# Softmax sums in an attention and two-layer MLP kernel: transposed before VectorE inverts them, with a new table of planned times

## The chip, the cores and the metric

The kernel runs on one core of a Trainium2 chip. The metric is the device time of one execution in microseconds (us). TensorE (PE in the profile) multiplies matrices, VectorE (DVE), ScalarE (ACT) and GpSimd (POOL) work on elements, SyncE (SP) issues the DMAs.

## What is computed

Attention over 4 batches x 8 heads, 576 positions, head size 64, with a rotary embedding on q and k; then two dense layers with their own activations, 2304 tokens, model width 512, inner width 2048.

```python
scores = scale * q_rot @ k_rot.T
scores = scores - max(scores, axis=-1)
attn = exp(scores)
attn = attn / (sum(attn, axis=-1) + 1e-09)
x = (attn @ v) reshaped to [2304, 512]
h = x @ w_in;   x = (h - tanh(h)) @ w_out
h = x @ w2_in;  out = (h * sigmoid(1.702 * h)) @ w2_out
```

All is float32; each product is made of products of rounded high and low parts, so most operands are split into two tiles.

## The kernel before

**Attention.** Heads are worked on in 16 pairs. For each pair, GpSimd makes the rotary embedding of q and k in four passes over a 128x1152 tile (`rope`, L484 and L486, and `qk_lo`, L527), and SP copies the halves to where TensorE wants them. Scores come in 9 units (`scores`, L561) into two PSUM tiles `sp`. VectorE takes the row maximum of each (`rowmax`, L567), ScalarE the exponential and, in the same instruction, the row sum (`expo`, L573), which goes to one column of the tile `sum`, 128 rows by 9 columns for a pair. TensorE transposes the exponentials (`etrans`, L591 to L604); ScalarE casts each transposed block to its high part (`evac`, L626, tile `eh`), VectorE subtracts that from the block and gets the low part (L624, tile `el` or a part of `eh`). TensorE multiplies both with v (`pv`, L640), ScalarE or VectorE copies the result out of PSUM (`pv_out`, L649 and L651, tile `xt`), and SP stores it.

**The sums.** The output is not divided at once. Five steps make the factor 1 / (sum + 1e-9) of every row and store it in DRAM: `r_add` (L664, ScalarE, adds 1e-9 to the 128x9 tile), `r_inv` (L667, VectorE, inverts it), `r_trans` (L671, TensorE, transposes it to 9x128 in the PSUM tile `ps_r`), `r_copy` (L677 on VectorE or L679 on ScalarE, copies it to the tile `rw`), `r_save` (L685 and L686, three DMAs to `rs`). Much later `x_fetch` (L862) reads the factors back, spread over partitions, and GpSimd multiplies the attention's output with them (L874) while it makes the first layer's input.

**The dense layers.** From about 282 us on, TensorE works through the two layers: `up` (L836), `down` (L941), and the second layer's products (L1138, L1179, L1265, L1322), with the activations on ScalarE and VectorE and the splits of their results on GpSimd. The weights of the first layer are converted from 64-bit words on the way (L325, L334, L336, L341, L345), partly during attention.

**What sets the order.** Every step is an `op` with a priority, the engines that may run it with a modelled duration, what it reads and writes, and the buffers it holds. The planner (`Plan.order`) runs them through a model of the engines before the program is traced, and the order that comes out is fixed: each instruction is held behind the one before it on its engine. The priorities of the steps of pair n are `PER * n + OFF[step]`; those of the first eight weight conversions are in `CT`. An op with `port=True` on VectorE is kept from overlapping GpSimd's in the model; others are not.

Of the kernel before, what the change touches and what calls it, by code (L numbers as in the profile page):

```python
# [34 lines left out]
}  # L35
PER = 14.87
# [11 lines left out]
CT = (41.4, 75, 90, 105, 120, 135, 150, 159.7)  # L48
# [149 lines left out]
def _cost(eng, dur):  # L198
    return eng, dur - LAP[eng], dur
# [3 lines left out]
def attention_moe_kernel(ctx: ExitStack, tc, qk, v, w1_in, w1_out, w2_in, w2_out, rope_tab, eye, out):  # L203
# [273 lines left out]
    def engine():  # L477
        return nc.vector if cur[0].eng == "DVE" else nc.gpsimd
# [184 lines left out]
    def r_add(n):  # L663
        nc.scalar.activation(st["sum", n], st["sum", n], AF.Identity, bias=1e-9)  # L664

    def r_inv(n):
        nc.vector.reciprocal(st["sum", n], st["sum", n])  # L667
# [5 lines left out]
    def r_copy(n):  # L673
        rw = st["rw", n] = ap.tile([9, 128], F32, tag="rw", name="rw", bufs=1)
        p = st.pop(("rt", n))[0:9, 0:128]
        if cur[0].eng == "DVE":
            nc.vector.tensor_copy(rw, p)  # L677
        else:
            nc.scalar.copy(rw, p)  # L679
# [43 lines left out]
    for n in range(NP):  # L723
        t0 = PER * n

        def at(k):
            return t0 + OFF[k]

        def bind(fn, *a, n=n):
            return lambda: fn(n, *a)  # L730
# [64 lines left out]
        for h in range(2):  # L795
            for part in range(2):
# [6 lines left out]
                for stage in range(3):  # L803
# [3 lines left out]
                    if stage == 0:  # L807
# [10 lines left out]
        op(at("rt"), bind(r_add), [_cost("ACT", 0.23)], [("e", n, i) for i in range(9)], [("ra", n)], [("sum", n)])  # L818
        op(at("rt"), bind(r_inv), [_cost("DVE", 0.215)], [("ra", n)], [("ri", n)], [("sum", n)])
        op(at("rt"), bind(r_trans), [("PE", 0.11, 0.27)], [("ri", n), "ident"], [("rt", n)], [("bank", "r", n), ("sum", n)])  # L820
        late_ops.append(op(at("rt"), bind(r_copy), [_cost("ACT", 0.25), _cost("DVE", 0.25)], [("rt", n)], [("rw", n)],
                           [("bank", "r", n), ("rw", n)]))
# [764 lines left out]
```

## Time and profile before

| | |
|---|---|
| median of 3 runs | 1064.37 us (1063.09 to 1064.77) |
| the profiled execution's own time | 1063.46 us |
| its span, first to last instruction | 1061.7 us |
| busy: PE, DVE, ACT, POOL | 98%, 65%, 68%, 73% of the span |
| granted TensorE clock | 0.999 |

Busy time is the union of an engine's instructions. A matmul's end is modelled and overlaps the next one, so a busy PE is not PE at its peak. A share over the whole span mixes attention, where all engines work, with the dense layers, where PE alone is full: read the stages apart.

### The profile page before, as it was taken

To read this page: it belongs to the slowest core of one execution; us is meant where nothing else is said; L and a number is where in the kernel's file an instruction comes from. 1 tells how busy PE (TensorE), PEld (TensorE's weight loads), DVE (VectorE), ACT (ScalarE), POOL (GpSimd) and SP (SyncE) were. 2 spreads that over 40 slices of the span, in tenths; PEclk is the share of its full clock that TensorE was granted. 3 is DMA by queue.
4 is the path that set the end of the run, shared out by engine and by line. 5 is a ranking of instruction groups with operands and counts; after the bars stand their busy time and mean duration, and the time that the engine had idled before them with its cause. 6 is when DMAs were issued, how large, how long until landed. Compare 5 with 4: busy or idle time off the path is not lost.

```text
span 1061.7 us, 19352 instructions
## 1 busy us (share of the span) xinstructions
PE 1038.3 (98%) x6578; PEld 998.7 (94%) x6578; DVE 693.8 (65%) x1243; ACT 719.7 (68%) x1623; POOL 780.1 (73%) x667
## 2 busy tenths in 40 slices
PE   5999999999999999999999999999999999999998
PEld 3898899998999999999999999998888999999998
DVE  7899898899787887777677776654121333562335
ACT  5999999989887776667767776743545444544442
POOL 2888899989356669869978868933933779977763
PEclk9999999999999999999999999999999999999999
DMA  8868778768433326655756578487468676777621
GB/s 280 281 237 308 260 277 281 259 224 294 152 99 120 105 96 214 209 193 191 243 189 227 189 259 308 156 308 280 157 221 340 233 291 224 263 283 266 232 99 60
DMA packets 107188, 236.36 MB, mean 223 GB/s; under 512 B 11729, under 2 KB 61137, under 8 KB 100049
## 3 DMA queue, kind: packets, MB, share of 16 engines
q1 hardware_dynamic: 107088, 235.12, 63.8%
q8 instruction: 52, 0.85, 0.3%
q14 instruction: 48, 0.39, 0.1%
HBM read 157.42 MB, written 49.36 MB: 195 GB/s over the span
## 4 chain that ended last, share of the span: by engine, by line
PE 77%; DVE 7%; ACT 5%; POOL 4%; DMA 3%; issue 3%; SPq 1%; DVEq 0%; ACTq 0%; POOLq 0%
PE ps_h L836 18%; PE y L941 18%; PE ps_h L1138 17%; PE y L1265 10%; PE y L1179 6%; DVE mx L567 2%; PE sp L561 2%; DVE el L624 2%; ACT e L573 2%; PE ps_o L640 2%; PE y L1322 2%; POOL qk L484 1%; PE ps_e L598 1%; ACT eh L626 1%; DMA st<-in_moe_w_out_dram 1%
## 5 line engine op out<-in xcount | busy, mean ns | idle before, releaser
L836 PE MATMUL ps_h<-xh,w 128*128 128x384 f32 x768 | 210.8, 336 | 0.2 <-ACT u L906 0.2
L1138 PE MATMUL ps_h<-xo,ws 128*128 128x384 f32 x1008 | 201.3, 341 | 0.0
L941 PE MATMUL y<-gh,w 128*128 128x384 f32 x768 | 195.6, 336 | 0.0
L1138 PEld LDWEIGHTS ps_h<-xo,ws 128*128 128x128 f32 x1008 | 173.5, 188 | 8.1 <-ACT su L1148 2.1
L836 PEld LDWEIGHTS ps_h<-xh,w 128*128 128x128 f32 x768 | 140.1, 188 | 0.7 <-ACT u L906 0.5
L941 PEld LDWEIGHTS y<-gh,w 128*128 128x128 f32 x768 | 139.0, 188 | 0.0
L928 POOL TENSOR_TENSOR gl<-t,gh 128x384 fp32r<-128x384 f32 x96 | 97.8, 1019 | 42.7 <-ACT gh L926 33.9
L941 PE MATMUL y<-gl,w 128*128 128x384 f32 x384 | 129.0, 336 | 0.0
L836 PE MATMUL ps_h<-xl,w 128*128 128x384 f32 x384 | 128.8, 335 | 0.0
L1296 DVE TENSOR_TENSOR sum<-y,sum 128x256 f32<-128x256 f32 (+1 forms) x108 | 54.0, 537 | 112.8 <-PE y L1265 112.8
L561 PE MATMUL sp<-kt,qt 128*128 128x288 f32 x624 | 115.8, 313 | 1.5 <-ACT e L573 0.9
L573 ACT ACTIVATE e<-sp,mx 128x576 f32<-128x576 f32 x144 | 107.5, 747 | 12.8 <-DVE mx L567 11.6
L567 DVE TENSOR_REDUCE mx<-sp 128x1 f32<-128x576 f32 x144 | 107.2, 748 | 4.8 <-PE sp L561 3.2
L624 DVE TENSOR_TENSOR el<-ps_e,eh 128x512 fp32r<-128x512 f32 x144 | 96.5, 684 | 14.3 <-ACT eh L626 13.4
L626 ACT CAST eh<-ps_e 128x512 fp32r<-128x512 f32 (+2 forms) x208 | 101.7, 532 | 4.6 <-PE ps_e L602 2.0
L910 DVE SCALAR_TENSOR_TENSOR w<-z,ps_h 128x384 f32<-128x384 f32 x96 | 52.8, 550 | 78.5 <-ACT t L903 78.2
L926 ACT CAST gh<-t 128x384 fp32r<-128x384 f32 x96 | 49.3, 513 | 70.9 <-DVE t L918 60.7
L561 PEld LDWEIGHTS sp<-kt,qt 128*128 128x128 f32 x624 | 87.9, 189 | 9.1 <-ACT e L573 7.7
L640 PE MATMUL ps_o<-eh,vw 128*128 128x256 f32 (+1 forms) x320 | 91.1, 307 | 3.5 <-DVE el L624 2.6
L1400 POOL TENSOR_TENSOR ex<-t,g2h 128x384 fp32r<-128x384 f32 x72 | 72.2, 1019 | 25.3 <-ACT g2h L1397 25.3
L1265 PE MATMUL y<-ws,g2h 128*128 128x256 f32 x486 | 90.1, 283 | 0.0
L1265 PE MATMUL y<-ws,ex 128*128 128x256 f32 x345 | 80.7, 282 | 0.0
(143 smaller groups left out, 2525.0 us busy)
## 6 DMA issues: line engine op xcount, KB each, us to landing
ws<-w SPq DMA_DIRECT2D x48, 1024.0 KB
w<-part SPq DMA_DIRECT2D x40, 512.0 KB
kt<-qk SPq DMA_DIRECT2D x64, 288.0 KB
ws<-w SPq DMA_DIRECT2D x24, 768.0 KB
qk<-in_qk_dram SPq DMA_DIRECT2D x30, 576.0 KB
st<-in_moe_w_in_dram SPq DMA_DIRECT2D x32, 512.0 KB
st<-in_moe_w_out_dram SPq DMA_DIRECT2D x32, 512.0 KB
qt<-qk SPq DMA_DIRECT2D x64, 144.0 KB
```

The source lines that it names most:

```text
L561: nc.tensor.matmul(sp[:, half, 0:HS], lhsT=w, rhs=m[:, half * HS:(half + 1) * HS], start=(o == 0), stop=(o == len(ops) - 1))
L567: nc.vector.tensor_reduce(mx, st["sp", n, i], axis=AX.XY, op=ALU.max, negate=True)
L573: nc.scalar.activation(e.rearrange("p (a b) -> p a b", a=2), st.pop(("sp", n, i)), AF.Exp, bias=st.pop(("mx", n, i)), accum_out=st["sum", ...
L624: nc.vector.tensor_sub(lo, src, hi.bitcast(F32))
L626: nc.scalar.copy(hi, src)
L640: nc.tensor.matmul(p[:, 0:wd], lhsT=w[:, h, kc].rearrange("p d a -> p (d a)"), rhs=m, start=(o == 0), stop=(o == 8))
L836: nc.tensor.matmul(p, lhsT=wi[:, a, kk, :], rhs=xx[:, kk, :], start=(o == 0), stop=(o == 11))
L928: nc.gpsimd.tensor_sub(gs[i][1], g, gs[i][0].bitcast(F32))
L941: nc.tensor.matmul(y, lhsT=w[:, a, cols], rhs=g, start=first and o == 0, stop=last and o == 2)
L1138: nc.tensor.matmul(hq[q, b], lhsT=wt(lw, k), rhs=x[:, 2 * lx + k], start=n in (1, 7) and c == 0, stop=n in (2, 3, 4) and c == 5, skip_grou ...
L1265: nc.tensor.matmul(y[:, x:x + 256], lhsT=g[:, cols], rhs=ws[q, s][:, a + l, o:o + 256], start=not own and m == 0, stop=m == 2 and (not own ...
L1400: engine().tensor_sub(l, g, h.bitcast(F32))
```

## The change

The sums are transposed first, and VectorE inverts the 9x128 tile from PSUM straight into `rw`. The copy is gone. The addition of 1e-9 may now run on VectorE too. The tables `OFF`, `PER` and `CT` have other numbers; two lines of them are shown.

```diff
-    "pv01": 23.03, "pv11": 27.36, "pv10": 29.03, "rt": 26.05, "dx": 25.11,
+    "pv00": 18.99, "pv01": 22.94, "pv11": 27.46, "pv10": 31.19, "rt": 18.15, "dx": 22.0,
...
-PER = 14.87
+PER = 14.83
...
-CT = (41.4, 75, 90, 105, 120, 135, 150, 159.7)
+CT = (52.6, 76.2, 89.5, 91.8, 122.9, 134.7, 153.2, 166.8)
...
     def r_add(n):
-        nc.scalar.activation(st["sum", n], st["sum", n], AF.Identity, bias=1e-9)
-
-    def r_inv(n):
-        nc.vector.reciprocal(st["sum", n], st["sum", n])
+        if cur[0].eng == "ACT":
+            nc.scalar.activation(st["sum", n], st["sum", n], AF.Identity, bias=1e-9)
+        else:
+            engine().tensor_scalar(st["sum", n], st["sum", n], 1.0, 1e-9, op0=ALU.mult, op1=ALU.add)
 
     def r_trans(n):
         p = st["rt", n] = bank(("bank", "r", n), "ps_r")
         nc.tensor.transpose(p[0:9, 0:128], st["sum", n], ident)
 
-    def r_copy(n):
+    def r_inv(n):
         rw = st["rw", n] = ap.tile([9, 128], F32, tag="rw", name="rw", bufs=1)
-        p = st.pop(("rt", n))[0:9, 0:128]
-        if cur[0].eng == "DVE":
-            nc.vector.tensor_copy(rw, p)
-        else:
-            nc.scalar.copy(rw, p)
+        nc.vector.reciprocal(rw, st.pop(("rt", n))[0:9, 0:128])
...
-        op(at("rt"), bind(r_add), [_cost("ACT", 0.23)], [("e", n, i) for i in range(9)], [("ra", n)], [("sum", n)])
-        op(at("rt"), bind(r_inv), [_cost("DVE", 0.215)], [("ra", n)], [("ri", n)], [("sum", n)])
-        op(at("rt"), bind(r_trans), [("PE", 0.11, 0.27)], [("ri", n), "ident"], [("rt", n)], [("bank", "r", n), ("sum", n)])
-        late_ops.append(op(at("rt"), bind(r_copy), [_cost("ACT", 0.25), _cost("DVE", 0.25)], [("rt", n)], [("rw", n)],
-                           [("bank", "r", n), ("rw", n)]))
+        op(at("rt"), bind(r_add), [_cost("DVE", 0.15), _cost("ACT", 0.22)], [("e", n, i) for i in range(9)], [("ra", n)], [("sum", n)])
+        op(at("rt"), bind(r_trans), [("PE", 0.11, 0.27)], [("ra", n), "ident"], [("rt", n)], [("bank", "r", n), ("sum", n)])
+        late_ops.append(op(at("rt"), bind(r_inv), [_cost("DVE", 0.28)], [("rt", n)], [("rw", n)], [("bank", "r", n), ("rw", n)]))
```

Because the planner runs anew, all engines have another order; the first 30 rows of VectorE's and of ScalarE's are the same as before. Over the whole program the instructions of the engines are the same but for these: on VectorE, 16 inversions of 128x9 become 16 of 9x128, 2 copies of `rw` go, 15 additions come, and 24 copies of `xt` become 30 (14 to 16 of 128x256, 10 to 14 of 128x320); on ScalarE, 16 additions become 1, 14 copies of `rw` go, 40 copies of `xt` become 34 (18 to 16 and 22 to 18), and 6 casts of `vw` 128x640 become 8; on GpSimd 10 roundings of `vw` become 8.

On VectorE in the eighth pair, before: the tile `sum_1981` holds the pair's sums, `mx` is a row maximum over a score tile `sp`, `el` and `eh` are the low parts of transposed blocks.

```order
L624 TENSOR_TENSOR el_2127<-ps_e_2221,eh_2126 128x2x256
L567 TENSOR_REDUCE mx_2255<-sp_2238 128x1
L624 TENSOR_TENSOR eh_2243<-ps_e_2234,eh_2243 64x256
L667 RECIPROCAL sum_1981<-sum_1981 128x9
L567 TENSOR_REDUCE mx_2281<-sp_2263 128x1
L624 TENSOR_TENSOR el_2244<-ps_e_2275,eh_2243 128x512
```

VectorE touches the sums once. The same place after the change, where `sum_1979` are the sums and `rw_2227` the factors:

```order
L624 TENSOR_TENSOR el_2120<-ps_e_2176,eh_2119 128x4x128
L667 TENSOR_SCALAR sum_1979<-sum_1979 128x9
L649 COPY xt_2214<-ps_o_2186 128x256
L624 TENSOR_TENSOR eh_2119<-ps_e_2193,eh_2119 64x256
L675 RECIPROCAL rw_2227<-ps_r_2217 9x128
L567 TENSOR_REDUCE mx_2229<-sp_2207 128x1
L567 TENSOR_REDUCE mx_2245<-sp_2220 128x1
L624 TENSOR_TENSOR el_2120<-ps_e_2231,eh_2119 128x2x256
```

VectorE now touches them twice, two instructions apart, and both row maxima of the score tiles in flight stand behind the inversion. TensorE in the same pair, before:

```order
L598 MATMUL ps_e_2315<-ident_84,e_2218 128x128
L671 MATMUL ps_r_2323<-ident_84,sum_1981 9x128
L561 MATMUL sp_2326<-kt_1999,qt0_135 128x288 x8
L561 MATMUL sp_2342<-kt_1999,qt0_135 128x288 x4
L640 MATMUL ps_o_2354<-eh_2126,vw_1923 128x320
```

The transposition of the sums came after the blocks `ps_e` of the next units. TensorE after the change:

```order
L640 MATMUL ps_o_2186<-eh_2019,vw_1921 128x256
L561 MATMUL sp_2207<-kt_2009,qt0_135 128x288 x4
L671 MATMUL ps_r_2217<-ident_84,sum_1979 9x128
L561 MATMUL sp_2220<-kt_2009,qt0_135 128x288 x4
L598 MATMUL ps_e_2231<-ident_84,e_2108 128x128
```

It stands now between the two score units whose row maxima stand behind the inversion on VectorE.

## Rows read from the trace of the kernel before

**Rows 1.** The page, section 1: busy us of each engine over the span.

```profile
PE 1038.3 (98%) x6578; PEld 998.7 (94%) x6578; DVE 693.8 (65%) x1243; ACT 719.7 (68%) x1623; POOL 780.1 (73%) x667
```

**Rows 2.** Windows: stretch, length, busy us of PE, PEld, DVE, ACT, POOL; clock, DMA.

```profile
20.00:282.00 262.00, 254.33 (x1908) 235.73 (x1908) 234.97 (x398) 245.36 (x602) 222.86 (x126) 1.00 0.77 263
282.00:1040.00 758.00, 757.76 (x4514) 740.57 (x4513) 430.64 (x790) 461.76 (x997) 549.54 (x533) 1.00 0.61 212
```

**Rows 3.** Windows again, the densest 40 us of VectorE's share in attention.

```profile
40.00:80.00 40.00, 38.64 (x300) 36.54 (x300) 36.42 (x62) 38.22 (x93) 33.60 (x16) 1.00 0.73 253
```

**Rows 4.** Waits of VectorE, 20 to 282 us: total, times, longest (us).

```profile
DVE el L624 <- ACT eh L626: 12.6, 29, 0.9
DVE eh L624 <- ACT eh L626: 5.3, 7, 1.4
```

**Rows 5.** Waits of ScalarE, 20 to 282 us.

```profile
ACT e L573 <- DVE mx L567: 10.7, 28, 0.8
```

**Rows 6.** Groups of VectorE by form: count | busy us, mean ns | idle before.

```profile
L567 DVE TENSOR_REDUCE mx<-sp 128x1 f32<-128x576 f32 x144 | 107.2, 748 | 4.8 <-PE sp L561 3.2
...
L649 DVE COPY xt<-ps_o 128x256 f32<-128x256 f32 x14 | 5.8, 416 | 0.1
...
L649 DVE COPY xt<-ps_o 128x320 f32<-128x320 f32 x10 | 4.8, 476 | 0.0
...
L667 DVE RECIPROCAL sum<-sum 128x9 f32<-128x9 f32 x16 | 3.4, 212 | 0.3
...
L677 DVE COPY rw<-ps_r 9x128 f32<-9x128 f32 x2 | 0.5, 274 | 0.0
...
L449 DVE CAST qt<-zero 128x128 fp32r<-128x128 f32 x2 | 0.4, 223 | 0.0
L519 DVE TENSOR_REDUCE even<-ident 128x1 f32<-128x64 f32 x1 | 0.2, 210 | 0.0
```

**Rows 7.** Groups of ScalarE by form, 20 to 290 us.

```profile
L651 ACT COPY xt<-ps_o 128x320 f32<-128x320 f32 x22 | 9.3, 421 | 0.6 <-PE ps_o L640 0.2
...
L651 ACT COPY xt<-ps_o 128x256 f32<-128x256 f32 x18 | 6.7, 374 | 0.3 <-PE ps_o L640 0.3
...
L490 ACT CAST vw<-v 128x640 fp32r<-128x640 f32 x5 | 4.0, 795 | 0.0
L679 ACT COPY rw<-ps_r 9x128 f32<-9x128 f32 x14 | 3.5, 253 | 1.5 <-PE ps_r L671 1.4
L664 ACT ACTIVATE sum<-sum 128x9 f32<-128x9 f32 x16 | 3.4, 215 | 0.0
```

**Rows 8.** Timeline of VectorE around one inversion: start, length.

```profile
166.03 0.22 DVE L667 RECIPROCAL sum<-sum 128x9 f32<-128x9 f32 x1
166.16 0.70 DVE L567 TENSOR_REDUCE mx<-sp 128x1 f32<-128x576 f32 x1
```

**Rows 9.** Groups of GpSimd by form, 20 to 282 us.

```profile
L484 POOL TENSOR_TENSOR qk<-qk,tab 128x1152 f32<-128x1152 f32 x28 | 74.2, 2667 | 3.8 <-PE ps_e L598 2.0 <-DMA v<-in_v_dram 1.4
L486 POOL TENSOR_TENSOR qk<-qk 128x1152 f32<-128x1152 f32 x15 | 39.9, 2663 | 18.2 <-DVE qk L484 17.2
L527 POOL TENSOR_TENSOR qk<-qk 128x1152 fp32r<-128x1152 f32 x14 | 37.4, 2670 | 4.1 <-ACT qk L490 4.1
L546 POOL TENSOR_TENSOR vw<-v,vw 128x640 fp32r<-128x640 f32 x16 | 25.4, 1589 | 4.6 <-ACT vw L490 4.0
```

**Rows 10.** Timeline at 724 us: VectorE's instructions with two SBUF inputs beside GpSimd's.

```profile
723.84 0.41 DVE L1200 TENSOR_TENSOR tt<-tt 128x256 f32<-128x256 f32 x1
724.12 1.01 POOL L1167 TENSOR_TENSOR g2l<-t,g2h 128x384 fp32r<-128x384 f32 x1 [0.74 <-ACT g2h L1165]
724.18 1.23 DVE L1202 TENSOR_TENSOR tt<-tt 128x256 f32<-128x256 f32 x1
```

**Rows 11.** One line's instructions: ns min/median/max, first and last start.

```profile
L667 DVE RECIPROCAL sum<-sum x16: 202/215/217, 33.5 to 281.2; 128x9 f32<-128x9 f32 x16
```

**Rows 12.** The first layer's up products: ns min/median/max, first and last start.

```profile
L836 PE MATMUL ps_h<-xh,w x768: 334/336/440, 281.9 to 679.0; 128*128 128x384 f32 x192
```

8 rows, old and new, of the table OFF are left out of this document.

## The prediction

> **What bounds the kernel now.** The page first: over the whole span TensorE is 98% busy and no other engine above 73% [rows 1], which suggests that nothing on VectorE matters. The windows say otherwise [rows 2]. From 282 to 1040 us TensorE is busy 757.76 of 758 us: a wall, whose length this change does not touch, so whatever moves its start moves the end by as much. From 20 to 282 us, the attention, three engines are almost full together: ScalarE 245.36 of 262 us (93.6%), VectorE 234.97 (89.7%), GpSimd 222.86 (85%), and TensorE's 254.33 has the ends of matmuls modelled into it. The question is how long these 262 us become.
>
> The waits say how the engines hold each other. VectorE's idle time is 262 - 234.97 = 27 us, and 12.6 + 5.3 = 17.9 us of it is waiting for ScalarE's casts [rows 4]. ScalarE waits 10.7 us for row maxima of VectorE [rows 5]. So the two feed each other in a loop, and each is the late one at times. The first 20 us are the same in both orders but for a swap or two, and I leave them out.
>
> **The change part by part.** All durations are from the profiled execution; sums are made against its 1063.46 us, 0.91 us under the median of the three runs, 1064.37 us.
>
> *ScalarE loses work.* 15 additions go at 0.215 us, 14 copies of the factors at 0.253, 2 copies of xt at 0.374 and 4 at 0.421, and 2 casts of 128x640 come at 0.795 [rows 7]: -3.23 - 3.54 - 0.75 - 1.68 + 1.59 = **-7.6 us**, so 237.8 us remain. GpSimd loses two short roundings; I count nothing for it.
>
> *VectorE: what has a price in the rows.* 16 inversions of 128x9 go at 0.212 us, 2 copies at 0.274, and 2 + 4 copies of xt come at 0.416 and 0.476 [rows 6]: -3.39 - 0.55 + 2.74 = -1.2 us.
>
> *VectorE: the inversion of 9x128.* No row has it. The lower bound is the copy of the same shape from PSUM, 0.274 us. The upper one is the old inversion scaled by columns, 0.212 x 128 / 9 = 3.0 us. To choose I take the old one apart. The two reductions give VectorE's price per column: (748 - 210) / (576 - 64) = 1.05 ns, and 210 - 64 x 1.05 = 143 ns on top [rows 6]. The copy of 9x128 fits that (143 + 134 = 277 against 274), and so do the copies of 256 columns (143 + 269 = 412 against 416). The inversion does not: by that rate its 9 columns are worth 152 ns and it took 212. The 69 ns above the 143 are 7.7 ns a column. So 128 columns are an estimated 143 + 128 x 7.7 = **1.13 us**, four times the copy, and 16 of them 18.1 us. The reading against it is that a very short instruction has a floor near 0.21 us whatever it does; no row of VectorE has fewer than 64 columns beside this one, so that stays open and is a rival.
>
> [...]
>
> *VectorE: the addition.* One input and the output in SBUF, 9 columns: 143 + 9 x 1.05 = 0.152 us, 15 of them 2.3 us, if nothing holds it. The bound on the other side is a wait for GpSimd, which is a rival below.
>
> *Sum on VectorE.* -1.2 + 18.1 + 2.3 = +19.2 us of durations. An instruction's last part lies under the next one's first: the inversion is 0.22 us long, and its successor starts 0.13 us after it [rows 8], 0.08 to 0.09 us of overlap. There are 21 more instructions, so the busy time grows by 19.2 - 21 x 0.085 = **+17.4 us, to 252.4 us of 262**.
>
> *The wait that is added.* The inversion now waits for TensorE's transposition, and that for VectorE's addition, with one or two of VectorE's instructions between (in the eighth pair a copy of 0.416 us [rows 6] and one low part). Queued behind the inversion are the maxima of both score tiles in flight; ScalarE's exponentials wait for these, and the tiles are free for TensorE only then. So the extra microsecond falls where it stops three engines, not in a corner. The lower bound of its own price is nothing, where the transposition is in time; I put nothing in the sum for it, since VectorE's fullness below has room for such gaps. On SP the three DMAs per pair that store the factors stay, in other places; what reads them is GpSimd's multiplication, pairs later, so I cost that at nothing. If it were late, GpSimd, with 39 us idle in the stretch, would take it.
>
> *From load to time.* VectorE becomes the fullest engine. The fullest one of before, ScalarE, came to 93.6% of the stretch, the rest being waits that the loop needs. If VectorE packs as well, the stretch is 252.4 / 0.936 = 269.7 us, 7.7 more. Bounds: if it only packs as in its own densest 40 us, 36.42 of 40 [rows 3], it is 252.4 / 0.91 = 277, 15 more; if the new work falls wholly into its waits, 0. I take 7.7, since ScalarE's share is the one that a limiting engine has reached over the whole stretch. For the new order itself I put nothing: it was made with 0.28 us for the inversion. **Forecast: 1063.46 + 7.7 = 1071.0 us, rounded, with 1066 to 1078 as its own range.**
>
> **The rivals.**
>
> *The addition waits for GpSimd: 1082 us.* What the trace shows: at 724.18 us an instruction of VectorE with two SBUF inputs began 0.06 us after one of GpSimd's and took 1.23 us, where its like took 0.41 alone [rows 10]. The old inversion, with one SBUF input, was never held: 202 to 217 ns in 16 instances beside a busy GpSimd [rows 11]. The addition has one input as well, which speaks against. [...] GpSimd's 57 instructions of 2.67 us and 16 of 1.59 [rows 9] hold 58% and 10% of the 262 us; who comes at a random moment waits half their length, 0.58 x 1.33 + 0.10 x 0.79 = 0.85 us on average, and about 0.1 more for the shorter kinds. 15 x 0.94 = 14 us on VectorE. With half of it in idle time that is 1078, in full 1086.
>
> [...]
>
> *The inversion costs what the copy does: 1060 us, faster.* With the floor reading it is 0.274 us and VectorE grows by 17.4 - 16 x 0.86 = 3.7 us only, to 238.7, beside ScalarE's 237.8. The fullest engine then has 6.7 us less than before; by the same 93.6% the stretch is 255 us, 7 us shorter, and half of that, 1060, if waits rather than load decide. The point where it turns is a VectorE as full as ScalarE was, 245.4 us: 7 us less than I have, so an inversion of 0.69 us.
>
> *VectorE's waits swallow it: 1064 us, no change.* The 17.9 us that VectorE waits for casts shrink as ScalarE gets lighter, and 17.4 us of work fit in their place. Against it: the inversion sits in front of the maxima, not where the waits were.
>
> **How the numbers follow.** Forecast 0.45, wait for GpSimd 0.25, cheap inversion 0.17, swallowed 0.13. Slower by over 0.2% (2.1 us, about what a measurement of this kernel tells from no change): the first two, 0.70; same 0.13; faster 0.17. The range, 1060 to 1083 us, holds the forecast, the swallowed case and about half of each of the other two.
>
> **What would show it.** The inversion's group on VectorE: 1.1 us right, 0.3 wrong. Its busy time in attention: about 252 us, ScalarE's about 238, with ScalarE waiting longer for maxima than the 10.7 us of before. The addition's group: 0.15 us, or a median near 1 us with a maximum above 2 for the rival. The first up product, at 281.9 us now [rows 12], at about 289. The forecast is wrong if the inversion is long and that product starts no later.

## The result

The changed kernel takes 1079.45 us (median of 4 runs, 1078.69 to 1080.1), the kernel before beside it 1064.51 (1063.09 to 1064.77). The ratio is 1.0147, with a 95% interval of 1.0134 to 1.016: 15 us slower. The forecast was 7.5 us slower. The rival with the wait for GpSimd stood at 1082, which is the forecast's long inversion with the wait on top. Both happened.

The page of the changed kernel, span and section 1 (busy us of each engine over the span), answers to [rows 1]:

```profile
span 1077.9 us, 19392 instructions
...
PE 1042.9 (97%) x6578; PEld 1000.9 (93%) x6578; DVE 718.5 (67%) x1264; ACT 716.6 (66%) x1592; POOL 774.7 (72%) x661
```

VectorE has 718.5 - 693.8 = 24.7 us more work than before, ScalarE 3.1 less, and the span is 16.2 us longer. Where it grew is told by one line's first start, as in [rows 12], here of the changed kernel (ns min/median/max, first and last start):

```profile
L830 PE MATMUL ps_h<-xh,w x768: 334/336/445, 297.3 to 694.4; 128*128 128x384 f32 x192
```

The first up product begins at 297.3 us in place of 281.9, so 15.4 of the 16.2 us are lost in the attention. The windows agree with [rows 2] on the rest: TensorE is as full after 282 us as it was.

```profile
20.00:282.00 262.00, 243.39 (x1794) 224.22 (x1794) 242.45 (x392) 225.52 (x533) 215.49 (x118) 0.99 0.74 254
282.00:1040.00 758.00, 757.21 (x4515) 738.08 (x4514) 442.32 (x808) 471.32 (x1021) 540.54 (x523) 1.00 0.62 215
```

In the first window ScalarE, which was at 245.36 us, does only 225.52, and VectorE is now the fullest of the three that work on elements. The two new instructions of VectorE, each as one line's instructions. The addition is shown with those who waited for it (us, times):

```profile
L667 DVE TENSOR_SCALAR sum<-sum x15: 173/668/2082, 30.8 to 276.8; 128x9 f32<-128x9 f32 x15
...
  PE ps_r L671: 7.6, 11
  PEld ps_r L671: 5.0, 4
```

The inversion is shown with what VectorE waited for before it:

```profile
L675 DVE RECIPROCAL rw<-ps_r x16: 935/946/947, 32.4 to 295.3; 9x128 f32<-9x128 f32 x16
...
  PE ps_r L671: 0.2, 1
```

The inversion takes 935 to 947 ns in its 16 instances. The addition takes 173 at best and 2082 at worst, with the same tile of 128x9 each time. The group by form gives the sum of both over 20 to 282 us (busy us, mean ns):

```profile
L675 DVE RECIPROCAL rw<-ps_r 9x128 f32<-9x128 f32 x15 | 14.1, 941 | 0.5
L667 DVE TENSOR_SCALAR sum<-sum 128x9 f32<-128x9 f32 x15 | 11.7, 779 | 0.3
```

Unhindered, the 15 additions would be 15 x 0.174 = 2.6 us, so 11.7 - 2.6 = 9.1 us of them are waiting. For whom, the timeline shows at the longest one, VectorE first, then GpSimd (start, length):

```profile
224.35 0.41 DVE L649 COPY xt<-ps_o 128x256 f32<-128x256 f32 x1
224.85 2.08 DVE L667 TENSOR_SCALAR sum<-sum 128x9 f32<-128x9 f32 x1
226.97 0.42 DVE L624 TENSOR_TENSOR eh<-ps_e,eh 64x256 fp32r<-64x256 f32 x1
227.41 0.95 DVE L675 RECIPROCAL rw<-ps_r 9x128 f32<-9x128 f32 x1
```

```profile
224.29 2.62 POOL L527 TENSOR_TENSOR qk<-qk 128x1152 fp32r<-128x1152 f32 x1
226.87 0.99 POOL L872 TENSOR_TENSOR xl<-x,xh 128x384 fp32r<-128x384 f32 x1
```

GpSimd's rounding began 0.56 us before the addition and ended at 224.29 + 2.62 = 226.91; the addition ended at 224.85 + 2.08 = 226.93. It waited out the rest of GpSimd's instruction, though it has only one input. The timelines show the same for all 15: 11 additions began while a GpSimd instruction ran and ended 28 to 34 ns after that instruction did. Three met none, and one met the last 19 ns of one; these four took 173 to 175 ns.

The transposition of the sums on TensorE stood behind the addition. From the longest one, two stretches of the windows, in the order of [rows 2]:

```profile
225.10:226.99 1.89, 0.00 (x2) 0.00 (x1) 1.86 (x2) 0.87 (x2) 1.89 (x2) 1.00 0.12 25
227.16:230.57 3.41, 3.41 (x16) 3.30 (x16) 3.35 (x6) 1.83 (x5) 3.41 (x3) 0.50 0.67 254
```

TensorE did nothing for 1.89 us, and then its granted clock was 0.50 for 3.41 us. From 104.28 us on it was 0.50 for 3.41 us again, after 1.61 us in which TensorE did nothing (101.53 to 103.14) and the second longest addition (1966 ns) ended. In the kernel before the clock is 1.00 up to 1059.3 us, 2.4 us before its end. What these two falls cost was not measured by themselves; half of 2 x 3.41 us, 3.4 us of TensorE's time, is an estimate of the most.

The waits of ScalarE, 20 to 282 us, before and after, answer to [rows 5]:

```profile
ACT e L573 <- DVE mx L567: 10.7, 28, 0.8
ACT eh L626 <- PE ps_e L598: 1.6, 3, 1.1
ACT eh L626 <- PE ps_e L602: 1.6, 3, 0.7
```

```profile
ACT e L573 <- DVE mx L567: 20.5, 24, 3.0
ACT eh L626 <- PE ps_e L598: 7.0, 10, 1.3
ACT eh L626 <- PE ps_e L602: 6.0, 5, 2.8
```

Those of VectorE after the change answer to [rows 4]:

```profile
DVE el L624 <- ACT eh L626: 8.4, 15, 0.9
...
DVE eh L624 <- ACT eh L626: 1.3, 2, 1.0
```

ScalarE waits 20.5 us for row maxima in place of 10.7, and 13.0 us for TensorE's transposed blocks in place of 3.2. VectorE waits 9.7 us for casts in place of 17.9. The account of VectorE goes by the stretch from 20 us to the first up product. Before:

```profile
20.00:281.90 261.90, 254.23 (x1908) 235.63 (x1907) 234.97 (x398) 245.26 (x601) 222.76 (x126) 1.00 0.77 263
```

After:

```profile
20.00:297.30 277.30, 258.35 (x1908) 238.08 (x1908) 256.76 (x415) 239.16 (x568) 221.24 (x124) 0.99 0.72 246
```

VectorE has 21.8 us more work in it and is idle for 20.5 us in place of 26.9. So 21.8 - 6.4 = 15.4 us remain, the delay of the first up product. The other 2.9 of its 24.7 us lie behind it, where TensorE is full.

### The profile page after: what moved, and what is told of

The parts are those of the page before. It is cut to its first block, busy times and chain, and to the rows that moved or that the text cites. A ratio compares the mean times of both kernels' runs of the same rounds, so it can differ in the third digit from the quotient of the medians.

```text
span 1077.9 us, 19392 instructions
## 1 busy us (share of the span) xinstructions
PE 1042.9 (97%) x6578; PEld 1000.9 (93%) x6578; DVE 718.5 (67%) x1264; ACT 716.6 (66%) x1592; POOL 774.7 (72%) x661
## 5 line engine op out<-in xcount | busy, mean ns | idle before, releaser
L573 ACT ACTIVATE e<-sp,mx 128x576 f32<-128x576 f32 x144 | 107.5, 748 | 23.8 <-DVE mx L567 22.4
L626 ACT CAST eh<-ps_e 128x512 fp32r<-128x512 f32 (+2 forms) x208 | 103.7, 528 | 14.3 <-PE ps_e L598 7.3
L640 PE MATMUL ps_o<-eh,vw 128*128 128x256 f32 (+1 forms) x320 | 94.9, 315 | 1.9 <-DVE rw L675 1.7
L1394 POOL TENSOR_TENSOR ex<-t,g2h 128x384 fp32r<-128x384 f32 x71 | 71.6, 1021 | 23.8 <-ACT g2h L1391 23.8
```

What stands on the lines that cost most here:

```text
L573: nc.scalar.activation(e.rearrange("p (a b) -> p a b", a=2), st.pop(("sp", n, i)), AF.Exp, bias=st.pop(("mx", n, i)), accum_out=st["sum", ...
L626: nc.scalar.copy(hi, src)
L640: nc.tensor.matmul(p[:, 0:wd], lhsT=w[:, h, kc].rearrange("p d a -> p (d a)"), rhs=m, start=(o == 0), stop=(o == 8))
L1394: engine().tensor_sub(l, g, h.bitcast(F32))
```

## The experiments

Theory A: the addition's wait for GpSimd makes the loss. Theory B: the longer inversion makes it. Theory C: the new order, with the added hop from VectorE to TensorE and back, makes it. The first four runs keep the order of the change, instruction by instruction, on every engine, and change only what the addition or the inversion is (the last leaves the addition out). The kernel before took 1064.04 us in them.

**An addition that does not wait** (`e1_add_one_port`).

```diff
-            engine().tensor_scalar(st["sum", n], st["sum", n], 1.0, 1e-9, op0=ALU.mult, op1=ALU.add)
+            nc.vector.tensor_reduce(st["sum", n], st["sum", n].rearrange("p (a one) -> p a one", one=1), axis=AX.X, op=ALU.add)
```

> The addition on VectorE becomes a reduction over a dimension of length 1 (the sums go through unchanged, 1e-9 is left out), in the order of the changed kernel to the instruction. Theory A (the addition waits for GpSimd: 15 of them hold VectorE for 12.7 us in all where 2.6 would do, and this is the larger half of the loss): the reduction takes under 0.25 us in all 15 places, and the time falls by 7 to 10 us, to 1070 to 1072 us. Theory B (the long inversion in front of the row maxima is the loss): 3 us or less, 1076 us or more. Theory C (the new order and the way VectorE to TensorE and back is the loss, whatever the instructions cost): 1077 us or more.

Measured: 1070.88 us, ratio 1.0065 (1.005 to 1.008). The line's instructions:

```profile
L667 DVE TENSOR_REDUCE sum<-sum x15: 153/165/166, 30.4 to 266.7; 128x9 f32<-128x9 f32 x15
```

The same tile in the same places, and 166 ns at most, though 12 of the 15 began while a GpSimd instruction ran (GpSimd is busy for 219.00 us of the 262): what waited was the kind of instruction, not the tile. It is worth 8.6 us for 9.1 us of waiting, as theory A had it (the 12.7 us in its text are 11.7 by the group). Nearly half of the loss stays, so A alone is not it. The waits of ScalarE, 20 to 282 us, tell the two apart:

```profile
ACT e L573 <- DVE mx L567: 18.2, 23, 2.5
ACT eh L626 <- PE ps_e L598: 4.8, 10, 1.2
...
ACT eh L626 <- PE ps_e L602: 0.9, 3, 0.5
```

The wait for TensorE's blocks falls from 13.0 to 5.7 us, the wait for maxima stays at 18.2. The granted clock over these 262 us is 1.00, where it was 0.99 in the change.

This run is also the case that the forecast describes, a long inversion and an unhindered addition. It took 1070.88 us where 1071.0 were forecast, and its first up product begins at 288.5 us, forecast about 289:

```profile
L830 PE MATMUL ps_h<-xh,w x768: 334/336/444, 288.5 to 685.6; 128*128 128x384 f32 x192
```

**An inversion as short as the plan believes** (`e2_copy_for_inversion`).

```diff
-        nc.vector.reciprocal(rw, st.pop(("rt", n))[0:9, 0:128])
+        nc.vector.tensor_copy(rw, st.pop(("rt", n))[0:9, 0:128])
```

> The inversion of 9x128 becomes a copy of the same tile (the division is left out), same order. The instruction goes from 0.946 to 0.274 us in 16 places, 10.8 us of VectorE. Theory A: 5 us or less, 1074 to 1077 us, since the waits of the addition stay. Theory B: 8 to 11 us, 1069 to 1072 us. Theory C: 1077 us or more.

Measured: 1071.28 us, ratio 1.0071 (1.0055 to 1.0088). The line's instructions:

```profile
L675 DVE COPY rw<-ps_r x16: 268/278/280, 32.2 to 287.1; 9x128 f32<-9x128 f32 x16
```

8.2 us back for 16 x 0.67 = 10.7 us of durations, as theory B had it. B alone is not it either: the two are not rivals.

**Both** (`e3_both`: the two edits together).

> Both edits together (no 1e-9, no division), same order: what is left is the new order with the way VectorE, TensorE, VectorE at the price that the planner had in mind. Theories A and B, if they only differ in shares: 1061 to 1065 us, no worse than before. Theory C: 1070 us or more.

Measured: 1062.56 us, ratio 0.999 (0.9981 to 1.0), as expected of A and B together. The two parts add up, 8.6 + 8.2 = 16.8 against 16.9. With both gone the median is 1.5 us below the kernel before and the interval reaches 1.0, though ScalarE is lighter: what is left of a gain is hardly to be seen. ScalarE waits 11.4 us for maxima here in place of 18.2 in `e1_add_one_port`, so 6.8 us of that wait went with the inversion's length.

**The addition not issued** (`e4_no_add`).

```diff
-            nc.scalar.activation(st["sum", n], st["sum", n], AF.Identity, bias=1e-9)
+            return
         else:
-            engine().tensor_scalar(st["sum", n], st["sum", n], 1.0, 1e-9, op0=ALU.mult, op1=ALU.add)
+            return
```

> The addition is not issued at all (1e-9 left out), the inversion stays, same order otherwise. TensorE's transposition then waits for ScalarE's last sum alone. Theory A: 1 us less than with the reduction in its place, 1069 to 1071 us. Theory C (the hop from VectorE to TensorE itself costs): 3 us or more below the run with the reduction. Theory B: 1076 us or more.

Measured: 1068.68 us, ratio 1.0044 (1.0029 to 1.0059), 2.2 us below the run with the reduction, between the readings of A (1 us) and C (3 us or more). That is the most that an unhindered addition and its hop cost together, so theory C is a small part.

After these four the question was whether the order has a share. The planner had been told 0.28 us for the inversion, and that the addition may stand anywhere. The next four (kernel before: 1063.49 us) cross the code paths with the tables, tell the planner the truth, and try the addition's removal on the old path.

**Old path, new tables** (`e5_old_path_new_tables`: in the kernel before only `OFF`, `PER` and `CT` are the change's).

```diff
-PER = 14.87
+PER = 14.83
```

> The kernel before with only the change's three tables of numbers (the due times, the pair period, the times of the chunks), so that the planner orders the old path (add on ScalarE, inversion of 128x9, transpose, copy) by them; nothing of the computation changes. Reading 1, the 15 us came from two delays on VectorE, 8.6 us of waiting for GpSimd in the addition and 8.2 us of longer inversion, and the tables alone are worth nothing that shows: 1061 to 1068 us. Reading 2, the tables are a better order whose gain the two delays hid (the run without both delays was 1.5 us under the kernel before): 1056 to 1061 us. Reading 3, the tables suit the new path alone and cost the old one: over 1068 us.

Measured: 1067.07 us, ratio 1.0032 (1.002 to 1.0044), within reading 1. The tables gain nothing on the old path. They cost 3.6 us there, which also shows how much another order can move the time by itself.

**New path, old tables** (`e6_new_path_old_tables`: the tables the other way round).

```diff
-PER = 14.83
+PER = 14.87
```

> The changed kernel with the tables of numbers of the kernel before, so that the new path (addition on VectorE where the planner puts it, transpose, inversion out of PSUM) runs in an order made from the old due times; nothing of the computation changes. Reading 1, the two delays belong to the path and not to the order: 1074 to 1084 us, 12 to 18 us of waiting for GpSimd and long inversions as in the change, the first up product near 297 us. Reading 2, it was the new order that put the addition beside GpSimd's two-input work: with the old tables the 15 additions take under 0.4 us in the mean, and the time is 1068 to 1073 us.

Measured: 1086.81 us, ratio 1.0216 (1.0203 to 1.023), above what either reading gave. The addition, one line's instructions:

```profile
L667 DVE TENSOR_SCALAR sum<-sum x10: 166/1505/2607, 30.6 to 301.0; 128x9 f32<-128x9 f32 x10
```

Ten additions have a median of 1505 ns here. So the path brings the loss under either order. Its size goes in part by what the additions meet on GpSimd: they wait 13.2 us in sum against 9.1, 4.1 of the 7.4 us between the two runs. The rest of the difference is not explained.

**The planner told the true costs** (`e7_true_costs`).

```diff
-        op(at("rt"), bind(r_add), [_cost("DVE", 0.15), _cost("ACT", 0.22)], [("e", n, i) for i in range(9)], [("ra", n)], [("sum", n)])
+        op(at("rt"), bind(r_add), [_cost("DVE", 0.174), _cost("ACT", 0.22)], [("e", n, i) for i in range(9)], [("ra", n)], [("sum", n)], port=True)
...
-        late_ops.append(op(at("rt"), bind(r_inv), [_cost("DVE", 0.28)], [("rt", n)], [("rw", n)], [("bank", "r", n), ("rw", n)]))
+        late_ops.append(op(at("rt"), bind(r_inv), [_cost("DVE", 0.94)], [("rt", n)], [("rw", n)], [("bank", "r", n), ("rw", n)]))
```

> The changed kernel with the planner told what the profile shows: the addition at 0.174 us on VectorE and held off GpSimd's two-input work, or 0.22 us on ScalarE as before; the inversion at 0.94 us instead of 0.28. The planner then puts 15 of the 16 additions on ScalarE and one on VectorE; nothing of the computation changes. Reading 1, the delays are what counts, whoever plans: the wait for GpSimd goes (8.6 us in the run with the reduce), the inversion's 8.2 us stays, 15 additions of some 0.22 us come back on ScalarE: 1070 to 1074 us. Reading 2, what hurt was that the order was made for an inversion of 0.28 us, so that the work behind it came late unplanned: with the true cost in the plan the time falls to 1063 to 1068 us.

Measured: 1065.11 us, ratio 1.0014 (1.0005 to 1.0022), reading 2: 14.3 us below the change, although all 16 inversions still take their 945 ns. The planner puts 15 additions back on ScalarE and one on VectorE, where it does not wait. Its page, section 1, its window, and its wait for maxima:

```profile
PE 1039.2 (98%) x6578; PEld 999.2 (94%) x6578; DVE 706.0 (66%) x1249; ACT 718.1 (68%) x1605; POOL 777.1 (73%) x663
```

```profile
20.00:282.00 262.00, 253.19 (x1892) 234.34 (x1892) 244.16 (x400) 241.53 (x580) 218.78 (x121) 1.00 0.77 261
```

```profile
ACT e L573 <- DVE mx L567: 11.9, 25, 1.2
```

VectorE does 244.16 us in the window, more than in the change's 242.45, and ScalarE does 241.53 beside it and waits 11.9 us for maxima in place of 20.5.

**The kernel before without its addition** (`e8_before_no_add`: `r_add` returns at once).

> The kernel before with the addition of 1e-9 not issued (each row's sum of exponentials is at least 1, since the largest exponent is 0, so float32 loses it anyway); the order of the rest is the same, instruction by instruction. Reading 1, a delay on ScalarE or a hop of the chain sum, inversion, transpose counts as on VectorE: 16 additions of 0.22 us less, 3.5 us, and one hop from engine to engine less per pair; 1060 to 1062.5 us. Reading 2, ScalarE has room there (its busy share of 20 to 282 us is 94%, and it waits 10.7 us for VectorE's maxima) and the saved time ends in that wait: 1063 to 1065.5 us.

Measured: 1064.49 us, ratio 1.0008 (1.0 to 1.0016), reading 2. Nothing gained: ScalarE is busy for 1.6 us less from 20 to 282 us (243.74 in place of 245.36) and waits 1.1 us more for maxima (11.8).

The next four (kernel before: 1063.42 us) take the true costs apart.

**The addition's true cost alone** (`e11_true_cost_add`: the first of the two lines of `e7_true_costs`).

> The changed kernel with one of the two corrections of the run with true costs: the planner is told of the addition (0.174 us on VectorE and to be held off GpSimd's two-input work, or 0.22 us on ScalarE), while the inversion stays at 0.28 us in its plan; nothing of the computation changes. The run with both corrections gave 1065.1 us, 14.3 under the change, though its inversions still took 0.945 us. Reading 1, about 8.6 us of that was the wait for GpSimd and 6 the inversion's true place in the plan: 1069 to 1073 us. Reading 2, the wait for GpSimd and what it set off was nearly all, and a long inversion that the plan does not know of costs little once the additions are out of the way: 1064 to 1067 us.

Measured: 1071.28 us, ratio 1.0077 (1.0065 to 1.0089), reading 1. All 16 additions are on ScalarE.

**The inversion's true cost alone** (`e12_true_cost_inversion`: the second line).

> The changed kernel with the other correction alone: the inversion at 0.94 us in the plan instead of 0.28, the addition as in the change (0.15 us, free to stand beside GpSimd's work); nothing of the computation changes. Reading 1, each correction is worth its own part: some 6 us come back and the additions on VectorE still wait for GpSimd by some 8 us: 1071 to 1076 us. Reading 2, the wait for GpSimd is nearly all of the loss: 1077 to 1081 us. Reading 3, the plan finds VectorE fuller and puts the additions on ScalarE by itself: then the waits go too, and it is 1064 to 1067 us.

Measured: 1079.88 us, ratio 1.0153 (1.014 to 1.0166), reading 2 by its number. The addition:

```profile
L667 DVE TENSOR_SCALAR sum<-sum x12: 174/898/1934, 30.5 to 295.0; 128x9 f32<-128x9 f32 x12
```

A plan that knows the inversion gains nothing while 12 additions stay on VectorE: over the whole program their 11.9 us are 9.8 of waiting, as much as in the change.

**Both true costs, a copy for the inversion** (`e13_true_costs_copy`: the edit of `e2_copy_for_inversion` in the order of `e7_true_costs`).

> The kernel with both true costs in its plan, its order kept instruction by instruction, but with a copy out of PSUM (0.28 us) where the inversion of 9x128 stands (0.945 us); the division by the sums is left out. In the order of the change the same exchange was worth 8.2 us. Reading 1, the length of the inversion costs as much in any order, and it is 1056 to 1059 us. Reading 2, in an order that reckons with 0.94 us other work covers it, and the exchange is worth under 2 us: 1063 to 1066 us.

Measured: 1064.97 us, ratio 1.0012 (1.0004 to 1.0021). The exchange that gave 8.2 us in the change's order gives 0.1 here. That is reading 2: in this order, which reckons with 0.94 us, the long inversion is covered.

**Both true costs, no addition** (`e14_true_cost_no_add`: `r_add` gone from the plan, the transposition reads the exponentials' sums).

> The kernel with both true costs, and the addition of 1e-9 taken out of the plan altogether (float32 loses it, each sum being at least 1), so the transposition follows the exponentials directly. Reading 1, an instruction of 0.22 us on ScalarE and one hop less for each of 16 pairs show: 1060 to 1063 us, under both kernels. Reading 2, they do not, as in the kernel before without its addition, and it stays at 1064 to 1066.5 us.

Measured: 1066.23 us, ratio 1.0027 (1.0018 to 1.0036), reading 2. No gain. But this run tells load and order apart. Its page, section 1, and then that of the run with the reduction:

```profile
PE 1039.0 (98%) x6578; PEld 997.8 (94%) x6578; DVE 709.1 (67%) x1254; ACT 713.4 (67%) x1586; POOL 775.3 (73%) x661
```

```profile
PE 1040.3 (97%) x6578; PEld 998.5 (93%) x6578; DVE 709.2 (66%) x1264; ACT 717.1 (67%) x1592; POOL 775.7 (73%) x661
```

VectorE is equally busy in both, 709.1 and 709.2 us, and they are 4.6 us apart (4.0 if each is taken against the kernel before beside it). Up to the first up product it is equally busy too, 246.7 and 247.1 us, in stretches of 264.9 and 268.5.

The next four (kernel before: 1064.06 us) ask how much of this is the chance of one order.

**The order of `e11_true_cost_add` with a copy for the inversion** (`e16_e11_copy`).

> The order of the run with the addition's true cost alone (additions on ScalarE, inversion planned at 0.28 us, 1071.3 us), kept instruction by instruction, with a copy out of PSUM where the inversion stands, so that the instruction is as short as the plan believes; the division by the sums is left out. The run with both true costs differs from that order only by the plan, and is 6.2 us faster. Reading 1, those 6 us are the price of an inversion that is 0.67 us longer than planned: 1063 to 1066.5 us here. Reading 2, that order is poorer by chance, whatever the inversion takes (the new tables moved the old path by 3.5 us too): 1069 to 1072 us.

Measured: 1066.04 us, ratio 1.0018 (1.0009 to 1.0027), reading 1. An inversion longer than planned costs 5.2 us in this order; the one that was planned for cost 0.1 in the order of `e7_true_costs`.

**The order of `e12_true_cost_inversion` with additions that do not wait** (`e17_e12_one_port`: the edit of `e1_add_one_port`).

> The order of the run with the inversion's true cost alone (12 additions on VectorE that wait for GpSimd by 9.8 us in sum, 1079.9 us), kept instruction by instruction, with the additions on VectorE as a reduction over one element (0.165 us, which did not wait), and so without the 1e-9. Reading 1, in an order that knows the inversion's length only the wait for GpSimd is left, and it is all of the loss: 1064 to 1068 us, 12 to 15 us for 9.8 us of waiting. Reading 2, the wait costs what it did in the change's order, some 8.6 us, and the rest is the order: 1070 to 1073 us.

Measured: 1069.96 us, ratio 1.0053 (1.004 to 1.0066). The wait is worth 9.9 us for 9.8 us of it: nearest to reading 2, with a rest of 4.9 us above `e7_true_costs`. Beside `e1_add_one_port` the run shows a limit: both have unhindered reductions on VectorE, here the plan knows the inversion's length and there it does not, and the gain is only 0.9 us, which the intervals do not tell from nothing.

**True costs, old tables** (`e15_true_costs_old_tables`).

> The kernel with both true costs, planned with the tables of numbers of the kernel before; nothing of the computation changes. Without the true costs the old tables were 7.3 us slower on the new path than the new ones (1086.8 against 1079.5). Reading 1, that difference was the chance of which additions met GpSimd's instructions (13.2 us of waiting against 9.1), and with the additions out of the way the two tables are alike: 1063 to 1068 us. Reading 2, the new tables suit the new path for other reasons too, and it is 1070 us or more.

Measured: 1065.65 us, ratio 1.0014 (1.0005 to 1.0022), reading 1. With both true costs the old tables do as well as the new ones, so the 7.4 us between them on the new path go with what the plan did not know. How much of it was the additions and how much the inversion this run does not tell.

**The old path replanned without its addition** (`e9_old_path_no_add`).

> The old path (inversion of 128x9 at 0.212 us, transposition, copy) with the old tables, and the addition of 1e-9 taken out of the plan (float32 loses it, each sum being at least 1), so that the inversion follows the exponentials directly; a version that might be faster than both kernels. Reading 1, an instruction of 0.22 us on ScalarE and a hop less per pair show once the plan knows of them: 1059 to 1062 us. Reading 2, as in the two other runs without the addition they fall into waits: 1062.5 to 1066 us.

Measured: 1065.31 us, ratio 1.001 (1.0001 to 1.002), reading 2. Not faster than the kernel before.

The last two (kernel before: 1063.87 us) are on those 4.9 us.

**That order with the additions on VectorE not issued** (`e18_e12_no_add_issued`).

> The order of the run with the inversion's true cost alone, kept instruction by instruction, with the 12 additions on VectorE not issued at all (the 4 on ScalarE stay), so that the transposition follows the exponentials; what is left out is the addition of 1e-9 for 12 of 16 pairs. With these additions as unhindered reductions it took 1070.0 us, the plan with both true costs 1065.1. Reading 1, even an addition that does not wait costs something on VectorE, since the sums then go through its full queue before TensorE can transpose them: 1064 to 1067 us. Reading 2, that order is poorer for another reason: 1068 to 1070.5 us.

Measured: 1068.77 us, ratio 1.0044 (1.003 to 1.0057). Reading 2: 1.2 us are the additions, the rest is that order.

**All additions on VectorE as reductions, all costs true** (`e19_reduce_all_true`).

```diff
-        op(at("rt"), bind(r_add), [_cost("DVE", 0.15), _cost("ACT", 0.22)], [("e", n, i) for i in range(9)], [("ra", n)], [("sum", n)])
+        op(at("rt"), bind(r_add), [_cost("DVE", 0.165)], [("e", n, i) for i in range(9)], [("ra", n)], [("sum", n)])
```

> All 16 additions on VectorE as a reduction over one element (0.165 us, without the 1e-9), the inversion at 0.94 us in the plan, so that the plan knows every duration and no addition waits for GpSimd; planned anew. Reading 1, what a plan knows it covers, wherever the addition stands: 1063 to 1067 us, as with both true costs. Reading 2, the addition's place on VectorE costs some 4 to 5 us of its own, as the run with 12 reductions (1070.0) hints: 1068 to 1073 us.

Measured: 1067.85 us, ratio 1.0037 (1.0024 to 1.0049), between the two readings, 2.7 us above `e7_true_costs`. This plan knows every duration and no addition waits, so true costs alone do not make an order as good as that one.

**Load and time of the runs on the new path.** VectorE's busy time of the page, less the 693.8 us of [rows 1], beside the span less its 1061.7, both of one profiled execution, and the median less that of the kernel before beside it:

| run | inversion planned at | VectorE, us more | span, us more | median, us more |
|---|---|---|---|---|
| e3_both | 0.28, is a copy | 5.8 | 2.5 | -1.5 |
| e16_e11_copy | 0.28, is a copy | 5.9 | 3.1 | 2.0 |
| e4_no_add | 0.28, takes 0.945 | 13.8 | 5.1 | 4.6 |
| e11_true_cost_add | 0.28, takes 0.945 | 14.5 | 7.8 | 7.9 |
| e2_copy_for_inversion | 0.28, is a copy, additions wait | 14.9 | 7.8 | 7.2 |
| e1_add_one_port | 0.28, takes 0.945 | 15.4 | 7.0 | 6.8 |
| the change | 0.28, takes 0.945, additions wait | 24.7 | 16.2 | 14.9 |
| e6_new_path_old_tables | 0.28, takes 0.945, additions wait | 28.7 | 23.8 | 23.3 |
| e12_true_cost_inversion | 0.94, additions on VectorE wait | 23.5 | 15.4 | 16.5 |
| e17_e12_one_port | 0.94, additions on VectorE | 13.9 | 6.5 | 5.9 |
| e18_e12_no_add_issued | 0.94, additions on VectorE not issued | 12.3 | 5.6 | 4.9 |
| e19_reduce_all_true | 0.94, additions on VectorE | 13.9 | 5.2 | 4.0 |
| e13_true_costs_copy | 0.94, is a copy | 3.3 | 0.4 | 1.6 |
| e15_true_costs_old_tables | 0.94, additions on ScalarE | 9.9 | 2.2 | 1.6 |
| e7_true_costs | 0.94, additions on ScalarE | 12.2 | 2.1 | 1.6 |
| e14_true_cost_no_add | 0.94, no additions | 15.3 | 1.9 | 2.8 |

The profiled execution of `e3_both` was the slowest of its ten, so its median is the better figure. In the change's own order time goes nearly with VectorE's work: from `e3_both` to `e1_add_one_port` 8.3 us of the median for 9.6 us of work, from there to the change 8.1 for 9.3. The last three carry 10 to 15 us more and pay 2 to 3: their plans know of all of it. But so does the plan of `e19_reduce_all_true`, which pays 4, and `e18_e12_no_add_issued`, as busy as `e7_true_costs`, pays 4.9. So what the plan knows is not all of it.

What in such an order does this can be seen in one place, but was not tried by itself. In `e7_true_costs` both row maxima stand right behind the inversion in 12 of 16 pairs, in `e15_true_costs_old_tables` in 10 and in `e14_true_cost_no_add` in 7. In the order of `e12_true_cost_inversion` and in `e19_reduce_all_true` it is 6, in the change 4, in `e11_true_cost_add` 3. The eighth pair of the change, shown ahead of the prediction, is one of these 4 and not typical. The timelines of VectorE around one inversion, the first of `e7_true_costs`, the second of `e11_true_cost_add`:

```profile
183.13 0.94 DVE L675 RECIPROCAL rw<-ps_r 9x128 f32<-9x128 f32 x1
184.01 1.39 DVE L567 TENSOR_REDUCE mx<-sp 128x1 f32<-128x576 f32 x2
185.31 0.68 DVE L624 TENSOR_TENSOR el<-ps_e,eh 128x512 fp32r<-128x512 f32 x1
```

```profile
185.36 0.94 DVE L675 RECIPROCAL rw<-ps_r 9x128 f32<-9x128 f32 x1
186.22 0.68 DVE L567 TENSOR_REDUCE mx<-sp 128x1 f32<-128x576 f32 x1
186.93 0.42 DVE L624 TENSOR_TENSOR eh<-ps_e,eh 64x256 fp32r<-64x256 f32 x1
187.38 0.76 DVE L567 TENSOR_REDUCE mx<-sp 128x1 f32<-128x576 f32 x1
```

In the second a low part comes between, and the second maximum ends 2.78 us after the inversion began, 0.5 us later than in the first (2.27). ScalarE's wait for maxima over 20 to 282 us is 17.0 us in that run, 11.9 in the first.

## Why the prediction was right and wrong

The direction was right, and so was the place: attention grew, and the dense layers behind it only started later. The size was half of what came, because the sum held the addition's wait for GpSimd at nothing. Step by step:

- *The inversion.* Estimated 1.13 us, measured 0.946. The choice between the bounds was right, the method too: the old inversion's 212 ns were not a floor of short instructions, since a 9-column reduction takes 165 ns. From the two inversions the rate is an estimated (946 - 212) / (128 - 9) = 6.2 ns a column in place of 7.7, with 156 ns for the rest in place of 143; that one of them reads SBUF and the other PSUM is left aside in it. 16 inversions are 15.1 us in place of 18.1.
- *The cheap inversion* (1060 us) is out by the 946 ns alone. `e3_both` shows what it would have given had the additions not waited either: 1062.56.
- *The addition.* This is the step that failed: "143 + 9 x 1.05 = 0.152 us, 15 of them 2.3 us, if nothing holds it". They took 11.7 us, of which 9.1 were waiting for GpSimd. The wait was named, priced (0.94 us each; it is 0.61) and put aside as a rival, with a chance of 0.25 beside the forecast's 0.45. The rival had it on top of the forecast, at 1078 to 1086 us, and what it describes happened: the inversion was long and the addition waited, and the two add up (`e1_add_one_port`, `e2_copy_for_inversion`, `e3_both`). Removed, the wait gives 8.6 us back. In the forecast's own sum it stood at nothing; it belonged there, times its chance at least.
- *One input speaks against a wait.* It does not: with one input the addition took up to 2082 ns as a tensor_scalar, and at most 166 as a reduction of the same tile in the same places. What it is in a tensor_scalar that waits, no run shows.
- *From load to time.* With the measured sizes the sum is -1.2 + 15.1 + 11.7 - 1.8 of overlap = 23.8 us, and by the forecast's own conversion (234.97 + 23.8) / 0.936 = 276.5, 14.5 us more. The measured 15 are near it. By the windows VectorE grew by 21.8 us and packed 92.6% of the longer stretch, so a conversion by the fullest engine was fair for this order, to some 3 us. It is no law: `e14_true_cost_no_add` and `e1_add_one_port` have the same load and stand 4.6 us apart. That the forecast's case came out at 1070.88 against 1071.0 is in part luck: its inversions were 3.0 us too long in the sum, and with the measured ones the conversion gives (234.97 + 14.5) / 0.936 = 266.5, 4.5 us more, where 6.8 were measured.
- *The new order at nothing, since it was made with 0.28 us.* The order by itself was worth next to nothing (`e3_both`), so the term was right. The remark mattered in another way: two orders that were made for 0.28 us pay 5.2 and 8.2 us for the true length, and the one made for 0.94 where it was tried pays 0.1. The sum held that price as load and did not say that it hangs on the plan.
- *The added rendezvous at nothing.* Nearly right: VectorE waited 0.2 us for the transposition, and an unhindered addition with its hop costs 2.2 us at most (`e4_no_add`). It was TensorE that waited 12.6 us for the addition, and ScalarE behind it for its blocks. The picture of two maxima behind the inversion holds for 4 of the 16 pairs.
- *Swallowed by VectorE's waits.* Partly right: its idle time up to the first up product fell from 26.9 to 20.5 us, so 6.4 of the 21.8 us of new work did not show.

What stays open: why the order with the inversion's true cost and the additions on VectorE is 3.7 us poorer even when these are not issued (`e18_e12_no_add_issued` against `e7_true_costs`), and whether the two maxima in a row are what covers the inversion. A copy for the inversion in that poorer order, which would tell whether it covers the length, was not run. How much of the 8.6 us of the wait came through the two falls of TensorE's clock is open too. Another plan alone moved the old path by 3.6 us, so differences of that size between two orders are not explained here.

## What to carry to other kernels

Price a moved instruction on the engine that it lands on by its form and by its neighbours, not only by its size: the same 128x9 tile took 165 ns as a reduction and up to 2082 as a tensor_scalar beside GpSimd. A rival that rests on another instruction can come true together with the forecast; put its price into the sum, times its chance, before choosing the likeliest. Where a planner orders the work, compare the durations that it was told with those in the trace: 10.7 us of unplanned work cost 5.2 and 8.2 us in two orders here, and 0.1 in the one order that was planned with it and tried. A true duration in the plan is no warrant for a good order, as the runs with the additions on VectorE show.

## What was unexpected of the hardware

A tensor_scalar with one input of only 9 columns took up to 2082 ns beside GpSimd in place of 173 to 175, and ended 28 to 34 ns after GpSimd's instruction in all 11 cases where it had to wait. The reciprocal of 9x128 out of PSUM takes 946 ns where the copy of the same shape takes 278, an estimated 6.2 ns a column, and with 935 to 947 ns in its 16 instances it did not change with what GpSimd did. A TensorE that waited 1.89 us for the longest addition ran at 0.50 of its clock for 3.41 us afterwards. No version tried was faster than the kernel before by more than can be measured.
